# The output layer of a second MLP as seven block products, with its sums kept transposed

## The chip, the cores and the metric

The kernel runs on one core of one Trainium2 chip. The metric is the time of one execution on the device, in microseconds. Five engines work side by side, each through its own queue of instructions: TensorE (PE in the profile, with its weight loads as PEld), VectorE (DVE), ScalarE (ACT), GpSimd (POOL) and SyncE (SP), which here issues every transfer between HBM and SBUF. TensorE writes its results to PSUM, in banks of 128 x 512 numbers of 32 bits.

## The reference

Eight batches of 576 tokens go through an attention with 32 memory slots per head and then through two MLPs. All inputs come in 64 bits, and the arithmetic is carried to more than 32-bit matmul precision by splitting each operand into a high and a low part.

```python
x = attention(q, k, v, phi)                  # 4608 tokens x 512
h = x @ w_in                                 # 512 -> 2048
x = np.maximum(0.01 * h, h) @ w_out          # 2048 -> 512
gate = 1.0 / (1.0 + np.exp(-(x @ w_gate)))   # 512 -> 1536
val = x @ w_val                              # 512 -> 1536
out = (gate * val) @ w2_out                  # 1536 -> 512
```

## The kernel before

The first part (up to about 780 us) runs attention and the first MLP batch by batch. In the same time it converts the weights of the second MLP in the background (`stash_jobs`): each piece of 512 columns comes in as 64-bit words (`Piece`), is made a 32-bit number by ScalarE, VectorE and GpSimd, split into high and low, and stored to HBM, `w_gate` and `w_val` as `gvs`, `w2_out` as `w2s`. The result of the first MLP is stored transposed, as `x2s`.

The second MLP works on `PAIRS`: four pairs of 2 x 512 tokens and a fifth of 2 x 256 (`h` is 512 or 256). Its 1536 hidden features are cut into `NTH` = 3 parts `th` of `TH` = 4 blocks of 128. For each th there are four groups (`m2_group`: j = 0, 1; val = 0 for the gate, 1 for the value). A group multiplies a 2 x 2 block of weights with a 2 x 2 block of the input by the Strassen-Winograd scheme: seven products (`prod`) in place of eight. Each product is six matmuls: two halves of the contraction, and for each the three combinations high x high, low x high, high x low. The input's seven operands `xo` (block sums of x and their split) are made once per pair by `x_sums`, `x_hi` and `x_lo`. The weights' seven operands come from `gvs`, two to a tile `wt` of 512 KB (`w_load`, loaded whenever a tile comes free). The products land in PSUM banks `x`, `y`, `z`; ScalarE copies and VectorE additions put the four results together, the gate gets its sigmoid, and the value group multiplies with it and splits the product into `pt`.

The output layer (`m2_out`) follows the four groups of each th and is a plain product: for each chunk of 128 tokens, four blocks times three combinations accumulate 128 tokens x 512 features in a bank. The bank is copied (th = 0) or added (th = 1, 2) into `osum`; at the last th the chunk is stored by `store`. At the end of a stage the output weights of the next th, four tiles `w2t` of 512 KB, are loaded (`w2_load`). Between the chunks of a pair's last stage the next pair's `x_hi` and `x_lo` are issued (`between`), the low halves alternately to VectorE and GpSimd.

The order of the instructions is written out by hand: an engine does them as the program lists them. Memory is held in numbered slots: 16 slots `wo` (8 `pt` pairs, 4 `w2t`, 4 `osum`), 9 slots `vw` for `wt`; after the fourth pair seven more `wt` tiles are opened in the place of the x tiles, which are no longer wanted.

Of the kernel before, what the change touches and what calls it, by code (L numbers as in the profile page):

```python
# [119 lines left out]
def tile_kernel(  # L120
# [35 lines left out]
    NOP = 7  # L156
    NOPS = NF2 * NOP
    SCALE = 1.0 / float(D) ** 0.5

    const = ctx.enter_context(tc.tile_pool(name="const", bufs=1))  # L160
# [13 lines left out]
    w2s = dr.tile([P, NF2, 2, DM], F32, name="w2s")  # L174

    ident = const.tile([P, P], F32, name="ident")
    ones = const.tile([P, P], F32, name="ones")
    mask = const.tile([P, 4], F32, name="mask")
# [19 lines left out]
    class Piece:  # L198
# [12 lines left out]
        def a(self):  # L211
# [5 lines left out]
            self.k = cvp.tile([P, PC], F32, tag="k", name="k", bufs=4)  # L217
            nc.scalar.activation(self.y, w[:, :, 1].bitcast(F32), AF.Abs, scale=2.0 ** -3)
            nc.scalar.activation(self.k, w[:, :, 0], AF.Copy, scale=2.0 ** -27, bias=2.0 ** 25)
            if not self.late:  # L220
                self.sign()
            yield

        def sign(self):
            hi = self.raw.rearrange("p (n t) -> p n t", t=2)[:, :, 1]
            nc.scalar.activation(hi.bitcast(I32), hi.bitcast(F32), AF.Prelu, scale=2.0 ** -60, alpha=2.0 ** 120)  # L226

        def b(self):
            y = self.y
            nc.vector.tensor_scalar(y, y, 2.0 ** -18, 15359.998046875, op0=ALU.max, op1=ALU.min)  # L230
            if self.late:
                self.sign()
            yield
# [59 lines left out]
    def stash_jobs():  # L293
# [12 lines left out]
        def prep(key, o0):  # L306
            st = {}
            hl = {}

            def sums(n):  # L310
                fa, fb = (held[key, i].rearrange("p (a e f) -> p a e f", a=2, e=2) for i in range(2))
                a11, a12, a21, a22 = fa[:, :, 0], fa[:, :, 1], fb[:, :, 0], fb[:, :, 1]
                if n == 0:
                    t = ap_.tile([P, KD, HALF], F32, tag="pbuf", name="sums", bufs=1)
                    t = t.rearrange("p c f -> p (c f)")[:, 0:768].rearrange("p (k a f) -> p k a f", k=3, a=2)
                    s1, s2, s3, s4 = a21, t[:, 0], t[:, 1], t[:, 2]
# [11 lines left out]
            def hi(*ks):  # L328
                for k in ks:
                    hl[k] = cvp.tile([P, 2, 2, P], F32R, tag="k", name="hl", bufs=4)  # L330
                    nc.scalar.copy(hl[k][:, 0], st[k])
                    yield

            def lo(*ks):
                for k in ks:
                    t = hl.pop(k)
                    nc.vector.tensor_sub(t[:, 1], st[k], f32(t[:, 0]))
                    nc.sync.dma_start(out=gvs[:, o0 + k], in_=f32(t))
# [16 lines left out]
        def w2_job(fc):  # L355
            t = {}
            p, stages = conv(rows(w2_out, fc), lambda f: t.update(f=f))

            def hi():
                t["hi"] = cvp.tile([P, PC], F32R, tag="k", name="w2_hi", bufs=4)  # L360
                nc.scalar.copy(t["hi"], t["f"])
                nc.sync.dma_start(out=w2s[:, fc, 0], in_=f32(t["hi"]))
                yield

            def lo():
                t["lo"] = cvp.tile([P, PC], F32R, tag="k", name="w2_lo", bufs=4)
                nc.vector.tensor_sub(t["lo"], t["f"], f32(t["hi"]))
                nc.sync.dma_start(out=w2s[:, fc, 1], in_=f32(t["lo"]))
                yield

            return 3, p, stages + [hi, lo]

        for th in range(NTH):
            for j in range(TH // 2):
                for i, w in enumerate((w_gate, w_val)):
                    for e in range(2):
                        fc = TH * th + 2 * j + e
                        p, stages = conv(
                            w[:, fc * P:(fc + 1) * P].bitcast(U32).rearrange("(c p) f -> p c f", p=P),
                            lambda f, k=((th, j, i), e): held.update({k: f}),  # L380
                        )
                        yield (3 if e == 0 else 4), p, stages
# [482 lines left out]
    pt = []  # L865
    osum = []
    tmps = []
    n_tmp = [0]


    def x_open():
# [495 lines left out]
```

## Time and profile before

| | us |
|---|---|
| median of 3 executions | 1598.17 (1596.18 to 1598.4) |
| profiled execution, its own time | 1599.8 |
| its span, first to last instruction | 1597.9 |
| TensorE busy in the span | 1548.1 (97%) |
| VectorE busy | 818.9 (51%) |
| ScalarE busy | 707.0 (44%) |
| GpSimd busy | 431.1 (27%) |

Matmuls are pipelined: the duration of one in a list (389 ns for 512 columns) is longer than its share of the time. The distance between starts, read from the chain, is what counts. The granted clock of TensorE over the whole span is 0.990 of full speed.

### The profile page before, as it was taken

Reading aid. Unit: us, or ns where it says so; the run is one execution under the profiler, and the core shown is the slowest. Engines: PE = TensorE matmul, PEld = TensorE weight load, DVE = VectorE, ACT = ScalarE, POOL = GpSimd, SP = SyncE. Lnnn points to the kernel's source line nnn. Section 1 sums busy time; section 2 is a strip of 40 time slices with the busy share of each in tenths; the row PEclk is TensorE's granted clock in tenths of the full one; section 3 lists DMA queues with packets and bytes.
Section 4 is the critical chain, followed back from the end, with each engine's and each line's share of the span. In section 5 each row is a group of like instructions: output and inputs, shape, how many; then the busy total and the mean of one; then the engine's idle time right before and its main releaser. Section 6 shows DMA issues by size and latency. Waiting matters only on the chain.

```text
span 1597.9 us, 27449 instructions
## 1 busy us (share of the span) xinstructions
PE 1548.1 (97%) x10544; PEld 1358.2 (85%) x10544; DVE 818.9 (51%) x1426; ACT 707.0 (44%) x1602; POOL 431.1 (27%) x429
## 2 busy tenths in 40 slices
PE   4889999999999999999999999999999999999999
PEld 2677989989899998999988888888888888888898
DVE  6886444555554555432145475355535475255544
ACT  5875555665556555645333143223333133223332
POOL 2986344454455444533100020000200020000100
PEclk8799999999999999999999999999999999999999
DMA  9823554554556555323456447536557447537692
GB/s 301 283 53 85 142 142 138 164 140 141 155 153 186 140 160 155 106 82 109 143 162 223 142 152 235 194 111 223 195 162 223 143 149 236 169 109 224 224 395 77
DMA packets 203490, 268.66 MB, mean 168 GB/s; under 512 B 95072, under 2 KB 140128, under 8 KB 203360
## 3 DMA queue, kind: packets, MB, share of 16 engines
q1 hardware_dynamic: 203360, 266.92, 53.4%
q8 instruction: 83, 1.36, 0.4%
q14 instruction: 47, 0.39, 0.1%
HBM read 219.68 MB, written 47.19 MB: 167 GB/s over the span
## 4 chain that ended last, share of the span: by engine, by line
PE 82%; ACT 1%; DMA 1%; DVE 1%; issue 0%; POOL 0%; DVEq 0%; SPq 0%; ACTq 0%; POOLq 0%
PE acc L841 20%; PE oacc L1047 18%; PE ps_y L949 14%; PE ps_h L819 9%; PE ps_x L949 9%; PE ps_z L949 9%; PE ps_vw L789 1%; PE ps_kv L556 1%; DMA wt<-gvs 1%; PE ps_sc L631 0%; ACT gr L824 0%; ACT obuf L850 0%; DVE vw L801 0%; DVE t L536 0%; ACT raw L226 0%
## 5 line engine op out<-in xcount | busy, mean ns | idle before, releaser
L841 PE MATMUL acc<-gh,wo 128*128 128x288 f32 x2048 | 428.6, 301 | 3.2 <-ACT obuf L850 1.8
L841 PEld LDWEIGHTS acc<-gh,wo 128*128 128x128 f32 x2048 | 328.7, 189 | 27.3 <-issue 14.2
L188 POOL TENSOR_TENSOR gl<-gr,gh 128x288 fp32r<-128x288 f32 x250 | 217.9, 873 | 329.4 <-ACT gh L187 216.7
L841 PE MATMUL acc<-gl,wo 128*128 128x288 f32 x1024 | 304.9, 298 | 1.0 <-POOL gl L188 1.0
L1047 PE MATMUL oacc<-w2t,pt 128*128 128x512 f32 x1296 | 296.3, 389 | 0.0
L1047 PEld LDWEIGHTS oacc<-w2t,pt 128*128 128x128 f32 x1296 | 243.1, 188 | 50.3
L949 PE MATMUL ps_y<-xo,wt 128*128 128x512 f32 (+1 forms) x1080 | 252.0, 369 | 0.0
L949 PEld LDWEIGHTS ps_y<-xo,wt 128*128 128x128 f32 x1080 | 190.4, 188 | 33.8
L819 PE MATMUL ps_h<-at_hi,vw 128*128 128x288 f32 x1024 | 215.2, 298 | 3.5 <-ACT vw L187 2.7
L824 ACT ACTIVATE gr<-ps_h 128x288 f32<-128x288 f32 x256 | 105.4, 412 | 253.1 <-PE ps_h L819 228.9
L912 POOL TENSOR_TENSOR xo<-xr,xo 128x512 fp32r<-128x512 f32 (+1 forms) x16 | 23.0, 1458 | 671.0 <-ACT xo L908 671.0
L841 PEld LDWEIGHTS acc<-gl,wo 128*128 128x128 f32 x1024 | 193.9, 189 | 1.8 <-POOL gl L188 1.7
L819 PEld LDWEIGHTS ps_h<-at_hi,vw 128*128 128x128 f32 x1024 | 167.2, 191 | 5.0 <-ACT vw L187 3.6
L949 PE MATMUL ps_z<-xo,wt 128*128 128x512 f32 (+1 forms) x720 | 167.4, 368 | 1.0 <-DMA wt<-gvs 1.0
L949 PE MATMUL ps_x<-xo,wt 128*128 128x512 f32 (+1 forms) x720 | 167.5, 368 | 0.0
L819 PE MATMUL ps_h<-at_lo,vw 128*128 128x288 f32 x512 | 152.0, 297 | 0.0
L984 ACT CAST pt<-sg 128x512 fp32r<-128x512 f32 (+1 forms) x120 | 69.4, 578 | 182.1 <-DVE sg L977 182.1
L949 PEld LDWEIGHTS ps_z<-xo,wt 128*128 128x128 f32 x720 | 127.1, 189 | 23.5 <-DVE pt L981 1.2
L949 PEld LDWEIGHTS ps_x<-xo,wt 128*128 128x128 f32 x720 | 127.2, 188 | 22.9
L187 ACT CAST gh<-gr 128x288 fp32r<-128x288 f32 x256 | 111.8, 437 | 2.2
L819 PEld LDWEIGHTS ps_h<-at_lo,vw 128*128 128x128 f32 x512 | 97.4, 190 | 0.0
L996 ACT COPY tmp<-ps_x 128x512 f32<-128x512 f32 (+1 forms) x60 | 32.4, 541 | 136.7 <-PE ps_x L949 136.7
(176 smaller groups left out, 1703.1 us busy)
## 6 DMA issues: line engine op xcount, KB each, us to landing
wt<-gvs SPq DMA_DIRECT2D x210, 512.0 KB, 4.5
w2t<-w2s SPq DMA_DIRECT2D x60, 512.0 KB, 5.1
gvs<-hl SPq DMA_DIRECT2D x84, 256.0 KB, 2.5
x2s<-obuf SPq DMA_DIRECT2D x15, 576.0 KB, 3.8
win<-in_moe_w_in_dram SPq DMA_DIRECT2D x16, 512.0 KB, 9.7
wo_bits<-in_moe_w_out_dram SPq DMA_DIRECT2D x16, 512.0 KB, 10.4
xr<-x2s SPq DMA_DIRECT2D x16, 512.0 KB, 6.3
out_dram<-osum SPq DMA_DIRECT2D x32, 256.0 KB, 2.0
```

Of the source, the lines that this page charges most:

```text
L187: nc.scalar.copy(hi, raw)
L188: eng.tensor_sub(lo, raw, f32(hi))
L556: nc.tensor.matmul(p[M * h:M * h + M, 0:2 * D], a, x, start=(c == 0), stop=(c == CC))
L789: nc.tensor.matmul(ps[g][M * h:M * h + M, n * VB:(n + 1) * VB], kvT[b, g][D * g:D * g + D, 1, M * h:M * h + M], win[j][D * g:D * g + D, h, ...
L819: nc.tensor.matmul(p[:, :HALF], w, x, start=(n == 0), stop=(n == 3 * NG - 1))
L824: nc.scalar.activation(gr, p[:, :HALF], AF.Prelu, alpha=0.01)
L841: nc.tensor.matmul(a[d][:, :HALF], w[:, ds_], x, start=(open_ and n == 0), stop=(close and n == 2),)
L912: eng.tensor_sub(t[:, 1, :h], x_operand(n, k, a), f32(t[:, 0, :h]))
L949: nc.tensor.matmul(bank, w[:, l, a, :], x[:, r, :h], start=(start and i == 0), stop=(i == 5), skip_group_check=not start,)
L984: nc.scalar.copy(d[:, 0, :h], s)
L996: read(lambda: nc.scalar.copy(s1, x))
L1047: nc.tensor.matmul(bank[i], pt[2 * f + t][:, l, q * P:(q + 1) * P], w2t[f][:, r, :], start=(f == 0 and l + r == 0), stop=(f == TH - 1 and ...
```

## The change

- **Output layer.** `m2_out` also uses seven products. The weights of `w2_out` are prepared as seven block operands by the same `prep` as the others (`out_blocks`), with 32-column blocks interleaved, and stored in `w2s` so that one block of one product (256 KB: two j, high and low, 128 x 128) is one load. The weights are now the stationary operand and the tokens the moving one: a stage is 7 products x 2 halves (e) x 6 matmuls of h columns, with results of 128 features x h tokens, the transpose of what is stored.
- **Ring.** Four tiles of 256 KB (`ring`) are loaded in the order of use; each is loaded again right after the bank that used it. They take two slots `wo`; the 14 operands `ops` take the other 14. The sums take four slots `vw`, which leaves five for `wt`.
- **Operands.** A value group now writes seven operands per j (four products, three differences more) and splits them: `op_hi` on ScalarE, `op_lo` on VectorE, spread over the following banks by `after`. For the last group of a pair (`direct`) more of it is issued at once.
- **Running chains.** In a group, `y` takes products 0, 1, 4, 6 one after another without being cleared, and ScalarE copies its contents after 0, 1 and 4; `z` takes 2 and 5. In the output stage banks 0 and 1 take products 0, 1, 4, 6, banks 2 and 3 products 2 and 5, and then 3. Each content is copied or added into `sums` (`SUM_OF`).
- **Order.** The stage of th - 1 comes after the first group of the next th; the stage of the last th follows its groups at once. `x_sums` moves from the groups into the first th's stage, `x_hi` and `x_lo` into the last ten banks of the last stage, 11 of 14 low halves on GpSimd.
- **Output.** VectorE turns the sums back in blocks of 32 x 32 (`turns`: 16 instructions per pair of 1024 tokens), one at a time after banks and two at a time in gate groups (`lazy`), and four stores of 128 KB with runs of 512 bytes bring 256 tokens out. For this the rows of q in the first batch are read as (c p) in place of (p c).
- **First MLP.** `gh`, `gl` and `gr` become slices of fixed tiles; constants move into another pool; late pieces convert their low word one step later.

Not shown in the diff: the pools, the helper `ghl_next`, the slots of the temporaries, and the group's branches for `direct`.

```diff
-    w2s = dr.tile([P, NF2, 2, DM], F32, name="w2s")
+    IN_AT = IN_SEQ = (0, 2, 1, 3, 4, 5, 6)
+    OUT_SEQ = (0, 2, 1, 5, 4, 3, 6)
+    w2s = dr.tile([P, NTH, 2, NOP, TH // 2, 2, P], F32, name="w2s")
...
+        def out_blocks(x, y):
+            x, y = (t.rearrange("p (g i e r) -> p i e g r", i=2, e=2, r=32) for t in (x, y))
+            return x[:, 0], y[:, 0], x[:, 1], y[:, 1]
...
-                out=s["q"][:, c], in_=q[b, g, :, 0:SM, :].rearrange("h (p c) d -> c p h d", c=CC)[c],
+                out=s["q"][:, c], in_=q[b, g, :, 0:SM, :].rearrange("h (c p) d -> c p h d", c=CC)[c],
...
+    def w2_load(t):
+        x = next(r_next, None)
+        if x:
+            th, e, k = x
+            nc.sync.dma_start(out=f32(t), in_=w2s[:, th, e, k])
+            r_at.append(t)
+
+    def read(*todo, turns=0):
+        for op in todo:
+            op()
+        n_read[0] += 1
+        for op in later.pop(n_read[0], []):
+            op()
+        for _ in range(turns):
+            if lazy:
+                lazy.pop(0)()
...
         y = ps_a.tile([P, 512], F32, tag="a", name="ps_y")[:, :h]
-        prod(1, y, True)
-        u2 = new()
-        read(lambda: nc.vector.tensor_add(u2, y, s1))
+        prod(0, y, True)
+        read(copy(c11, y), turns=turns)
         yield
         z = ps_h.tile([P, 512], F32, tag="h", name="ps_z")[:, :h]
         prod(2, z, True)
+        read(copy(c22, z), turns=turns)
+        yield
+        prod(1, y, False)
+        read(copy(c12, y), turns=turns)
+        yield
+        x = ps_h.tile([P, 512], F32, tag="h", name="ps_x")[:, :h]
+        prod(3, x, True)
+        read(add(c11, x, c11), turns=turns)
...
+        for k in OUT_SEQ:
+            for e in range(2):
+                start = k in (0, 2, 3)
+                b = banks[e if k in (0, 1, 4, 6) else 2 + e][:, :h]
+                w = r_at.pop(0)
+                i = 0
+                for j in range(TH // 2):
+                    for l, r in ((0, 0), (0, 1), (1, 0)):
+                        nc.tensor.matmul(
+                            b, w[:, j, l, :], ops[j][k][:, r, :h], start=(start and i == 0), stop=(i == 5),
+                            skip_group_check=not start,
+                        )
+                        i += 1
+                w2_load(w)
+                o = sums[SUM_OF[k]][:, e, :h]
+                if th == 0 and k in (0, 2, 1, 6):
+                    read(lambda: nc.scalar.copy(o, b), turns=1)
+                else:
+                    read(lambda: nc.vector.tensor_add(o, b, o), turns=1)
+                for f in between.pop(0) if between else ():
+                    f()
...
+                        if th > 0 and (j, val) == (0, 0):
+                            sums_ = [] if th > 1 or not more else [(n + 1, a, i) for a in range(2) for i in range(4)]
+                            m2_out(n, th - 1, [[]] * 5 + [[lambda o=o: x_sums(*o)] for o in sums_])
...
+            m2_out(n, NTH - 1, between)
+            if n + 2 == len(PAIRS):
+                w_free.extend(p2[0].tile([P, 2 * PC], F32R, tag="xr", name="wt", bufs=7) for _ in xr + xt)
+                w_load()
```

## Rows read from the trace of the kernel before

**Rows 1.** Windows: start:end, length, busy us (count) per engine, granted clock, DMA share, GB/s.
```profile
200.00:400.00 200.00, 195.06 (x1842) 182.43 (x1841) 102.38 (x198) 115.40 (x304) 95.76 (x104) 0.99 0.50 145
...
600.00:780.00 180.00, 179.20 (x1585) 170.92 (x1584) 59.79 (x111) 93.68 (x238) 76.45 (x84) 1.00 0.34 108
780.00:1498.10 718.10, 718.10 (x3179) 595.27 (x3179) 367.09 (x555) 218.21 (x380) 38.97 (x28) 1.00 0.56 179
1498.10:1597.90 99.80, 94.80 (x649) 88.10 (x647) 48.05 (x117) 28.99 (x76) 0.00 (x0) 1.00 0.67 256
```

**Rows 2.** Chain of waits, output stages: start us, length us, what.
```profile
818.14 21.76 PE oacc L1047 x96
877.98 21.76 PE oacc L1047 x96
...
1519.74 10.91 PE oacc L1047 x48
```

**Rows 3.** Chain of waits, 1490 to 1530 us, the fifth pair's first products.
```profile
1502.16 8.47 DMA wt<-gvs
1510.63 0.14 issue
...
1512.42 0.72 PE ps_y L949 x6
```

**Rows 4.** Transfers of the page: count, size, median us from issue to landing.
```profile
wt<-gvs SPq DMA_DIRECT2D x210, 512.0 KB, 4.5
...
out_dram<-osum SPq DMA_DIRECT2D x32, 256.0 KB, 2.0
...
ph<-in_phi_dram SPq DMA_DIRECT2D x16, 256.0 KB, 4.4
```

**Rows 5.** Transfers issued from 1017.4 to 1017.6 us.
```profile
w2t<-w2s SPq DMA_DIRECT2D x1, 512.0 KB, 3.6
```

**Rows 6.** SyncE's instructions in order, 1476 to 1530 us.
```profile
1476.41 0.32 SPq L918 DMA_DIRECT2D wt<-gvs  x1
...
1502.16 24.20 SPq L918 DMA_DIRECT2D wt<-gvs  x21
```

**Rows 7.** Transfers issued from 1502 to 1520 us.
```profile
wt<-gvs SPq DMA_DIRECT2D x16, 512.0 KB, 10.2
```

**Rows 8.** Windows of the fifth pair, columns as in rows 1.
```profile
1498.10:1519.74 21.64, 20.64 (x170) 20.45 (x169) 11.92 (x30) 7.79 (x21) 0.00 (x0) 1.00 0.92 342
1519.74:1530.65 10.91, 10.91 (x51) 9.02 (x50) 2.71 (x8) 2.98 (x6) 0.00 (x0) 1.00 1.03 410
```

**Rows 9.** VectorE's instructions in order, 1117 to 1140 and 1540 to 1552 us.
```profile
1118.57 0.68 DVE L977 TENSOR_TENSOR sg<-sg,tmp 128x512 f32<-128x512 f32 x1
1119.17 0.68 DVE L1030 TENSOR_TENSOR tmp<-ps_y,tmp 128x512 f32<-128x512 f32 x1
...
1126.11 0.68 DVE L1058 TENSOR_TENSOR osum<-oacc,osum 128x512 f32<-128x512 f32 x1
1126.71 1.19 DVE L912 TENSOR_TENSOR xo<-xt,xo 128x512 fp32r<-128x512 f32 x1
...
1541.75 0.42 DVE L977 TENSOR_TENSOR sg<-sg,tmp 128x256 f32<-128x256 f32 x1
1542.09 0.42 DVE L1030 TENSOR_TENSOR tmp<-ps_y,tmp 128x256 f32<-128x256 f32 x1
```

**Rows 10.** Groups by line and shape: busy us, mean ns of one, idle before.
```profile
L996 ACT COPY tmp<-ps_x 128x512 f32<-128x512 f32 x48 | 28.1, 586 | 114.1 <-PE ps_x L949 114.1
...
L912 POOL TENSOR_TENSOR xo<-xr,xo 128x512 fp32r<-128x512 f32 x12 | 19.5, 1651 | 503.1 <-ACT xo L908 503.1
...
L641 DVE STREAM_TRANSPOSE e<-ps_sc 128x288 f32<-128x288 f32 x28 | 13.0, 473 | 11.9 <-PE ps_sc L631 11.9
```

**Rows 11.** All engines in order, 1593 to 1598 us.
```profile
1592.83 1.07 PE L1047 MATMUL oacc<-w2t,pt 128*128 128x512 f32 x4
...
1593.93 0.69 DVE L1058 TENSOR_TENSOR osum<-oacc,osum 128x512 f32<-128x512 f32 x1 [0.67 <-PE oacc L1047]
```

## What I predict, and how the numbers come about

> **What bounds the kernel now.** I read the busy time of each engine by stage first. From 200 us on TensorE is busy nearly all the time: 195 of 200 us early in the first MLP, 718.1 of 718.1 us in the first four pairs of the second MLP and 94.8 of 99.8 us in the fifth pair, at a granted clock of 0.99 to 1.00 [rows 1]. VectorE and ScalarE are about half idle there (367 and 218 of 718 us). The chain of waits comes second: it shows how regular the second MLP is [rows 2]. An output stage of 96 matmuls takes 21.76 us, and the next one starts 59.84 us after the last, so 38.08 us hold the 168 matmuls of four groups. Both come to 226.7 ns for 512 columns, with no gap. In the fifth pair an output stage is 48 matmuls of 512 columns in 10.91 us, and six matmuls of 256 columns take 0.72 us [rows 3]: 120 ns each. So a matmul taken away is time taken away, as long as what feeds TensorE keeps up. The rest of the reading asks that: how fast VectorE and ScalarE work off a queue, and how fast a block of weights lands.
>
> **What the change removes from TensorE.** An output stage goes from 8 chunks x 4 x 3 = 96 matmuls to 7 products x 2 halves x 6 = 84 of 512 columns. Twelve stages in the first four pairs: 144 x 226.7 ns = **-32.6 us**. In the fifth pair the moving side is now 256 tokens wide: 144 matmuls at 227.3 ns (32.7 us) become 252 at 120 ns (30.2 us): **-2.5 us**. The groups keep their 168 matmuls.
>
> **The ring of output weights, first four pairs.** Four tiles of 256 KB take the place of four of 512 KB that were loaded a whole th ahead. The load for bank i+4 is issued when bank i's six matmuls are done, and has three banks, 3 x 1.36 = 4.08 us, to land. The trace has no such load. Its neighbours: a 256 KB store lands in 2.0 us, a 512 KB tile of group weights in 4.5 us [rows 4], the first of a burst of four output-weight loads, 512 KB, in 3.6 us [rows 5]; a landing reaches TensorE 0.14 us later [rows 3]. I take 2.9 us, about half way between 2.0 and 3.6: 3.04 us against 4.08, so **0**. Bounds: 0, and with 4.5 us 0.56 us late at the fifth, ninth and thirteenth bank of 12 stages, 36 x 0.56 = +20.
>
> The Trainium skill (DMA: Bandwidth & Descriptors, Anatomy of one DMA) gives a fixed 2.0 us or so and bytes over 436 GB/s for a transfer; by it, as an estimate, the load would take 2.6 us, which is nothing in this term and 4 us less in the next one. That the fixed part stays when the piece is halved speaks against this ring; the rows agree in that the 256 KB store still takes 2.0 us.
>
> **The ring, fifth pair.** A bank is 0.72 us there, so the cover is 2.16 us and a load of 2.9 + 0.14 us is 0.88 us late. Three late points in each of three stages, less the first, which is the next term: 8 x 0.88 = **+7.0**. Bounds: 0 at 2.0 us, 8 x 2.48 = +20 at 4.5 us.
>
> **The queue ahead of the fifth pair's first output stage.** When pair 3 ends, seven more tiles of group weights are opened and loaded at once, as before. Before, that filled the transfer engines: after 1502 us loads were issued back to back on SyncE [rows 6], each landed after 10.2 us [rows 7], and 410 GB/s moved while TensorE waited only 1.0 us of 21.64 [rows 8], because 16 tiles were held or on the way and no output weights were wanted in a hurry: the four of the next th had been asked for at the end of the stage before. After, the first output stage comes after five groups, 5 x 5.16 = 25.8 us (20.64 us for four [rows 8]), and its ring loads queue on SyncE behind everything issued by then: 7 tiles, 17.5 tiles freed by the five groups, and pair 3's output stores, which move from that pair's end into these groups. At 410 GB/s a tile costs 1.28 us: 24.5 x 1.28 + 2.1 MB / 410 GB/s = 31.3 + 5.1 = 36.4 us. The queue is 10.6 us behind when the stage begins, and its fifth bank waits about that long (the load's own landing and its cover cancel within 1 us): **+10.6**. Bounds: if the groups take 1 us longer each and the stores pass unnoticed, 0.5. The stores now go in runs of 512 bytes, and 256 KB of phi in such runs land in 4.4 us against 2.0 for a store in long runs [rows 4]: eight times 2.4 us more, less the queue's overlap, gives up to +25.
>
> **VectorE and ScalarE.** Per pair of 1024 tokens VectorE goes from 139 instructions (36 in each th's groups, 16 bank sums, 8 sums and 7 splits for the next pair) to 187 (42 in each th's groups, 34 bank sums, 16 transposes, 8 and 3), ScalarE from 94 (24 a th, 8 bank copies, 14 casts) to 136 (38 a th, 8, 14). In a queue that never empties VectorE starts a 512-column instruction every 0.605 us, a 256-column one every 0.34 us, and those that read PSUM are as fast beside a busy GpSimd (0.68 us), while a split between two SBUF tiles grows to 1.19 us [rows 9]. 187 x 0.605 = 113 us in a pair of 3 x 57.1 = 171 us; ScalarE at 0.59 us [rows 10] 80 us. On the mean both lie beside TensorE. The dense place is the last group of a pair, whose seven operands go straight into the output stage. From the fifth product's end at 6.8 us (the group's start is 0) VectorE has ten instructions until the third product's operand is split at 12.7 us; TensorE wants it at 13.1 us. Behind these, seven splits and differences and the first bank sums share the queue, and each bank is summed before it is wanted again. No stall by this count, 0.4 us of room. I take 0.5 us at each of five such places and 0.5 us elsewhere: **+3**. Bounds 0 and, at 2 us each, +10. GpSimd gets 11 of 14 splits of the next pair instead of 7, at 1.65 us apiece [rows 10]; they have 19 us of output stage and then a product of 1.36 us for every two.
>
> **Ends.** Before, 4.0 us pass from the last matmul (1593.9 us [rows 11]) to the span's end: a sum and a store. After: a sum (0.42 [rows 9]), four transposes of 256 columns (0.44 each by the 0.473 us of one of 288 [rows 10]), four store issues (0.32 each [rows 6]), the landing (2.0 [rows 4]) and some 0.5 us of hand-overs: 6.0 us, **+2.0**. The 1.0 us wait for weights at the fifth pair's start: **-1.0**.
>
> **First MLP.** Six preparations of output weights add 24 sums, 30 splits, 30 casts and 18 stores on VectorE, ScalarE and SyncE. VectorE is busy 102 of 200 us and 60 of 180 us there [rows 1]; some 27 us more in 540 us is hidden. 0, bounds -3 and +3. The other moves (slices of one tile in place of pools, the order in which q's rows of the first batch are read) leave every count as it was: 0.
>
> **Sum.** -32.6 - 2.5 + 0 + 7.0 + 10.6 + 3 + 2.0 - 1.0 = -13.5 us, against the profiled execution's own 1599.8 us: **1586.3 us**. That execution is 1.6 us above the median shown (0.1%), which is inside what I call no change: 0.2%, 3.2 us, is about what a measurement of this kernel can tell.
>
> **The rivals.**
> - *The queue does no harm* (0.22). The ring's loads find idle engines, the first stage waits 1 us, later banks 4 us in all, VectorE 1 us: -32.6 - 2.5 + 1 + 4 + 1 + 2 - 1 = -28 us, **1572 us**. For it: before, TensorE waited only 1.0 us in the same stretch. Against it: loads of 10.2 us there.
> - *The ring is late everywhere* (0.10), the other side: a 256 KB block lands no sooner than a 512 KB tile, at 4.5 us. Then +20 in the first four pairs and +13 more in the fifth: **1619 us**. It decides from a landing of 4.1 us. For it: 4.5 us in the same kind of stretch; against it: 3.6 us for the burst's first.
> - *The new chain on ScalarE and VectorE holds TensorE* (0.08): each accumulation into a running bank waits for a copy of what it held, behind whatever ScalarE waits for. 0.4 us in each of 60 groups is 24 us in place of 3: **1607 us**; slower from 0.3 us each. Against it: 47 to 66% load and 1.36 us between a copy and the next use.
> - *The fifth pair gives it all back* (0.16): stores in small runs cost the full +25: **1601 us**. The Trainium skill (TensorE: Matmul & The Clock Gate, Part 1) adds that an idle array falls from 2.4 to 1.2 GHz, so a wait of this length would be followed by matmuls at half speed; before, the granted clock stays 1.00 there, with no wait long enough to show it.
> - My sum as it stands (0.44), 1577 to 1597 us.
>
> **How the numbers follow.** 1586 us is the likeliest case. The range runs from 1567, below the first rival, to 1607: it leaves out the late ring, half of the chain and the lowest part of the first. Faster: nearly all of my case, the first rival and a quarter of the last, 0.68; same: half of the last and a little of mine, 0.10; slower 0.22.
>
> **What would show it.** Output stages of 84 matmuls in 19.0 us with a period of 57.1 us prove the first term and the ring's cover; a period near 58.8 us means the ring is late. The landing of the 256 KB loads decides: under 2 us the fifth pair is nearly free, at 3 us it has short waits every fourth bank. A wait of some 10 us at its first output stage, by TensorE for a ring block, is the queue. Waits of TensorE or of its weight loads for ScalarE would be the chain. I am wrong if the fifth pair takes under 105 us or the first four save less than 25 us.

## The result, and the profile after

The changed kernel takes 1609.38 us, the median of four executions (1607.29 to 1610.8), against 1598.29 us (1596.18 to 1598.76) for the kernel before beside it: a ratio of 1.0071, with an interval of 1.0053 to 1.0088. It is slower by 0.7%, and 2.4 us above the range that was given. The profiled execution took 1610.8 us, its span 1609.0 us (before: 1597.9), at a granted clock of 0.982 (before: 0.990).

The windows by stage come first, columns as in [rows 1]:

```profile
200.00:400.00 200.00, 192.80 (x1815) 179.19 (x1814) 110.75 (x220) 117.74 (x312) 97.05 (x102) 0.99 0.51 151
600.00:780.00 180.00, 177.66 (x1570) 168.98 (x1569) 72.89 (x130) 93.56 (x243) 77.66 (x86) 0.99 0.31 94
1477.50:1518.50 41.00, 28.11 (x212) 27.49 (x211) 21.78 (x62) 15.13 (x44) 0.00 (x0) 0.83 0.97 328
1518.50:1535.90 17.40, 12.56 (x86) 11.75 (x85) 2.94 (x8) 3.41 (x10) 0.00 (x0) 0.90 0.78 276
...
1557.40:1571.60 14.20, 10.91 (x86) 10.21 (x85) 5.90 (x15) 0.77 (x3) 0.00 (x0) 1.00 0.74 242
1571.60:1609.00 37.40, 28.11 (x212) 26.04 (x210) 22.79 (x62) 10.74 (x30) 0.00 (x0) 0.93 0.41 121
1479.50:1500.00 20.50, 7.97 (x54) 7.77 (x53) 5.02 (x15) 3.08 (x10) 0.00 (x0) 0.70 1.03 344
826.12:1477.50 651.38, 650.48 (x2856) 534.92 (x2856) 432.33 (x704) 286.35 (x512) 55.15 (x44) 1.00 0.67 214
```

The last line is the first four pairs from the end of their first four groups on, 651.4 us. Before, that end is the first output stage of [rows 2], 818.14, and the fifth pair's first product comes at 1498.1 [rows 1]: 680.0 us for the same groups and stages. TensorE still has no gap worth naming there: the one wait found for it is 0.4 us, for a ring block in the very first stage. The fifth pair, from 1477.50 to the end, takes 131.5 us where it took 99.8, and in the first four of its windows shown TensorE is busy for 69 to 77% of the time. The line of 1479.5 to 1500 us is the worst stretch of its first groups, at a granted clock of 0.70. In the two windows of the first MLP it is busy for about 2 us less than in [rows 1].

Where the first MLP ends is read from the matmuls of its last accumulator `acc` between 770 and 810 us: shapes, first and last start. The first line is of the changed kernel, the second of the kernel before:

```profile
L854 PE MATMUL acc<-ghl,wo x99: 288/296/311, 769.8 to 793.2; 128*128 128x288 f32 x99
```

```profile
L841 PE MATMUL acc<-gl,wo x20: 288/294/310, 770.6 to 785.2; 128*128 128x288 f32 x20
```

793.2 against 785.2: the first MLP ends 8 us later. The next mark agrees: the first four groups end at 826.12, which is the first output stage in the chain below (835.64) less one group of 9.52 us, since a fifth group now stands ahead of that stage; before it was 818.14.

The account of the spans: first MLP **+8.0**, first four pairs **-28.6**, fifth pair with its tail **+31.7**: +11.1 us, from 1597.9 to 1609.0.

The chain of waits in the first four pairs, columns as in [rows 2]:

```profile
835.64 1.38 PE oacc L1133 x6
...
893.40 19.04 PE oacc L1133 x84
...
1008.61 19.09 PE oacc L1133 x84
...
1065.78 19.04 PE oacc L1133 x84
```

A stage of 84 matmuls takes 19.04 us where [rows 2] shows 21.76 for 96, and from 1008.61 to 1065.78 the period is 57.17 us. The same view in the fifth pair, around its first groups and at its first output stage:

```profile
1479.02 8.25 DMA wt<-gvs
1487.28 6.42 DMA out_dram<-turned
...
1493.82 0.77 DVE turned L1120 x2
...
1496.65 1.65 PE ps_y L999 x6
1498.30 1.28 PE ps_x L999 x6
1499.58 1.29 PE ps_y L999 x6
...
1519.39 5.79 DMA ring<-w2s
```

SyncE's instructions at the first place, in order, show what the two transfers at 1479 and 1487 us are:

```profile
1478.11 3.90 SPq L937 DMA_DIRECT2D wt<-gvs  x7
1482.06 5.54 SPq L1173 DMA_DIRECT2D out_dram<-turned  x4
```

And the waits between 1478 and 1500 us (who waited for whom: us in total, times, longest):

```profile
DVE turned L1120 <- DMA out_dram<-turned: 13.6, 2, 12.8
ACT sg L1023 <- DVE tmp L1029: 13.5, 2, 13.0
PEld ps_y L999 <- ACT tmp L1032: 12.7, 1, 12.7
PE ps_y L999 <- ACT tmp L1032: 12.5, 1, 12.5
```

This is one wait handed on three times. The seven extra tiles of weights are issued first; the stores of the pair before are issued behind them and land late. There are two staging tiles `turned`, so VectorE's next transpose, issued in a gate group two at a time, stands still until a store has landed. Behind it on VectorE is an addition that ScalarE wants for the sigmoid, and behind that sigmoid on ScalarE is the copy of a bank that TensorE wants to reuse. TensorE stops for 12.5 us for a store with which it has nothing to do.

The transfers of the page:

```profile
ring<-w2s SPq DMA_DIRECT2D x210, 256.0 KB, 2.9
...
out_dram<-turned SPq DMA_DIRECT2D x72, 128.0 KB, 2.9
```

And the end, all engines in order:

```profile
1599.78 1.66 PE L1133 MATMUL oacc<-op,ring 128*128 128x256 f32 x12 [0.19 <-DMA ring<-w2s]
...
1601.81 1.74 DVE L1120 STREAM_TRANSPOSE turned<-sum 128x256 f32<-128x256 f32 x5
1602.27 3.92 SPq L1173 DMA_DIRECT2D out_dram<-turned  x8
```

The last matmul ends at 1601.4 us, the span at 1609.0: 7.6 us where it was 4.0.

### The profile page after: what moved, and what is told of

The parts are those of the page before. It is cut to its first block, busy times and chain, and to the rows that moved or that the text cites. A ratio compares the mean times of both kernels' runs of the same rounds, so it can differ in the third digit from the quotient of the medians.

```text
span 1609.0 us, 28276 instructions
## 1 busy us (share of the span) xinstructions
PE 1529.6 (95%) x10508; PEld 1339.6 (83%) x10508; DVE 953.4 (59%) x1724; ACT 820.1 (51%) x1846; POOL 449.4 (28%) x445
## 4 chain that ended last, share of the span: by engine, by line
PE 71%; DVE 6%; DMA 3%; ACT 3%; issue 1%; SPq 0%; DVEq 0%; ACTq 0%
PE acc L854 18%; PE ps_y L999 17%; PE oacc L1133 12%; PE ps_h L833 8%; PE ps_z L999 8%; PE ps_x L999 4%; DMA ring<-w2s 1%; PE ps_vw L803 1%; DVE op L1017 1%; DVE sum L1143 1%; PE ps_kv L570 1%; DVE sg L1020 1%; ACT op L1013 1%; DVE sg L1026 1%; DVE tmp L1029 1%
## 5 line engine op out<-in xcount | busy, mean ns | idle before, releaser
L854 PE MATMUL acc<-ghl,wo 128*128 128x288 f32 x3072 | 466.7, 301 | 6.4 <-POOL ghl L186 2.2
L854 PEld LDWEIGHTS acc<-ghl,wo 128*128 128x128 f32 x3072 | 424.3, 190 | 33.1 <-issue 13.4
L999 PE MATMUL ps_y<-xo,wt 128*128 128x512 f32 (+1 forms) x1440 | 330.1, 370 | 13.7 <-ACT tmp L1032 13.6
L186 POOL TENSOR_TENSOR ghl<-grs,ghl 128x288 fp32r<-128x288 f32 x250 | 217.8, 873 | 339.4 <-ACT ghl L185 256.5
L1133 PE MATMUL oacc<-op,ring 128*128 128x512 f32 (+1 forms) x1260 | 270.1, 372 | 10.5 <-DMA ring<-w2s 8.5
L1133 PEld LDWEIGHTS oacc<-op,ring 128*128 128x128 f32 x1260 | 221.0, 190 | 57.3 <-DVE sum L1143 8.0
L837 ACT ACTIVATE grs<-ps_h 128x288 f32<-128x288 f32 x256 | 105.5, 412 | 251.5 <-PE ps_h L833 223.3
L1143 DVE TENSOR_TENSOR sum<-oacc,sum 128x512 f32<-128x512 f32 (+1 forms) x170 | 106.8, 635 | 105.5 <-PE oacc L1133 104.7
L1013 ACT CAST op<-sg 128x512 fp32r<-128x512 f32 (+1 forms) x180 | 103.5, 579 | 77.1 <-DVE sg L1020 47.9
L185 ACT CAST ghl<-grs 128x288 fp32r<-128x288 f32 x256 | 111.7, 436 | 2.0
L1017 DVE TENSOR_TENSOR op<-sg,op 128x512 fp32r<-128x512 f32 (+1 forms) x180 | 111.6, 643 | 0.5
```

Of the source, the lines that this page charges most:

```text
L185: nc.scalar.copy(hi, raw)
L186: eng.tensor_sub(lo, raw, f32(hi))
L837: nc.scalar.activation(gr, p[:, :HALF], AF.Prelu, alpha=0.01)
L854: nc.tensor.matmul(a[d][:, :HALF], w[:, ds_], x, start=(open_ and n == 0), stop=(close and n == 2),)
L999: nc.tensor.matmul(bank, w[:, l, a, :], x[:, r, :h], start=(start and i == 0), stop=(i == 5), skip_group_check=not start,)
L1013: return lambda: nc.scalar.copy(ops[j][k][:, 0, :h], x)
```

## The experiments

Each ran beside the kernel before on its chip, whose medians were 1598.6 to 1600.0 us. Where one time is given, the kernel ran once, and its stages are read rather than its total: "first MLP" is the last start of `acc` against 785.2 us of before, and the fifth pair is split into its five groups ahead of the first output stage (ideal 25.8 us), its stages (ideal 10.1 us each) and the rest. In the changed kernel these are +8.0; 41.0; 17.4, 14.3; and 21.5 us for the last stage (13.9) with the tail.

**late_open.** The seven extra tiles are opened three groups into the fifth pair.

```diff
+    if (n + 1, th, j, val) == (len(PAIRS), 0, 1, 0):
+        w_free.extend(p2[0].tile([P, 2 * PC], F32R, tag="xr", name="wt", bufs=7) for _ in xr + xt)
+        w_load()
...
-            if n + 2 == len(PAIRS):
-                w_free.extend(p2[0].tile([P, 2 * PC], F32R, tag="xr", name="wt", bufs=7) for _ in xr + xt)
-                w_load()
```

> One edit: the seven extra weight tiles of the fifth pair are opened after its second gate group instead of before its first group. Theory A (the seven loads of 3.7 MB stand in the transfer queue ahead of pair 3's output stores; the stores free the two staging tiles late; VectorE's transposes wait for them and hold up everything behind them, 12.5 us of TensorE waiting for ScalarE): the 12.5 us wait shrinks to under 4 us and the low clock after it goes, so the fifth pair takes 115 to 120 us instead of 131.5 and the whole 1594 to 1599 us. Rival B (the stores themselves, in runs of 512 bytes and two staging tiles, are too slow whatever stands ahead of them): the wait stays above 8 us and the whole above 1603 us.

1611.3 us, no gain. The groups fell to 33.4 us and VectorE's long wait for a store from 12.8 to 2.5 us, so the mechanism was the one supposed; but the first stage grew to 24.3 us. Its chain:

```profile
1504.18 10.48 DMA wt<-gvs
...
1514.72 9.57 DMA ring<-w2s
...
1524.42 4.19 PE oacc L1133 x18
```

The ring's load now queues behind the moved tiles and holds TensorE for 9.8 us: the term that I had priced at 10.6 us, at the place where I had put it, though with the tiles opened three groups later than in the sum. The time was not saved, it changed its name.

**slow_turns.** In the fifth pair one transpose is issued after each product, in place of two in gate groups alone: `turns = 1 if n + 1 == len(PAIRS) else 0 if val else 2`.

> One edit: in the fifth pair's groups one lazy instruction (transpose or store) is issued after every product, in place of two after each product of gate groups. The seven loads stay where they are. Theory A: the transposes still come to a staging tile whose store stands behind 3.7 MB of weights; the wait is only moved by a few products, and 6 to 12 us of it stay: 1603 to 1609 us. Rival B (two transposes per 0.72 us product are simply too dense for VectorE): the wait is gone and the whole comes to 1594 to 1598 us.

1612.63 us, above both ranges, with the first MLP 11.3 us late; the groups stay at 41.0 us. TensorE's largest wait falls to 7.3 us and comes later, and smaller ones make up for it; VectorE still waits for the landing of a store (11.2 us at the longest). Spreading the transposes does not help while the stores land late.

**ring_deep.** Four of the seven tiles become eight more blocks of the ring, opened at the same point.

```diff
+                xs = [p2[0].tile([P, 2 * PC], F32R, tag="xr", name="wt", bufs=7) for _ in xr + xt]
+                for t in xs[:4]:
+                    t = t.rearrange("p (i j l f) -> p i j l f", i=2, j=TH // 2, l=2)
+                    for i in range(2):
+                        w2_load(t[:, i])
+                w_free.extend(xs[4:])
```

> One edit: of the seven extra tiles of the fifth pair four become eight more ring blocks (12 in place of 4) and three become weight tiles; they are opened at the same point as before. Theory (a 256 KB block takes 2.9 us to land against 2.16 us of cover, and queues behind weight tiles at the first stage): the three output stages of the fifth pair fall from 17.4, 14.3 and about 14 us to about 10.3 us each, 14 us less, so about 1595 us; the 12.5 us wait in the first group stays. Rival (the stages are late because VectorE's bank sums and the operands are late): the stages shrink by less than 4 us in all, 1605 us or more.

1595.81 us. Windows of its groups, its long wait and two of its stages:

```profile
1477.00:1517.40 40.40, 28.36 (x212) 27.90 (x211) 21.81 (x62) 15.02 (x44) 0.00 (x0) 0.83 0.96 329
1483.40:1495.50 12.10, 0.33 (x4) 0.13 (x2) 2.07 (x6) 1.20 (x4) 0.00 (x0) 0.67 1.06 388
1517.40:1527.50 10.10, 10.10 (x87) 10.10 (x86) 2.95 (x8) 3.42 (x10) 0.00 (x0) 1.00 1.04 398
1548.90:1559.00 10.10, 10.10 (x87) 10.10 (x86) 5.95 (x15) 0.82 (x3) 0.00 (x0) 1.00 0.98 348
```

With twelve blocks the stages are TensorE alone, busy for 10.10 of 10.10 us, and the last stage with the tail falls by 2.3 to 19.2 us. The long wait stays as it was, 12.1 us with the transfers at 1.06 busy. So the two losses of the fifth pair are separate: the ring's depth holds the stages, the stores behind the loads hold the groups.

**fifth_all.** The deep ring, opened three groups later, one transpose after each product, and two after each bank of the very last stage.

> Late opening, one lazy instruction after every product, twelve ring blocks, and two lazy instructions after each bank of the very last stage. If the fifth pair's excess is the queue (12.5 us and the low clock), the ring (14 us) and the tail (2 us), the pair goes from 131.5 to 101 to 106 us and the whole to 1579 to 1585 us, ratio to before 0.988 to 0.992. If the copies on ScalarE and the sums on VectorE bound its groups, the pair stays above 112 us and the whole above 1590 us.

1593.57 us over ten executions, ratio 0.9972 (0.9962 to 0.9982); 1579 to 1585 was expected. The stages are at their 10.07 us, but the groups still take 39.8 us, in several waits of 1 to 4 us for weights. The transfers are 98.5% busy from 1475 to 1515 us, where 13.3 MB pass.

**bare_w2.** The preparations of the output weights leave out their sums, casts and splits; the pieces are stored as they are, so that the output is computed from other weights.

```diff
-                yield 4, None, prep((th, j, i), blocks, dst)
+                yield 4, None, prep((th, j, i), blocks, dst) if i < 2 else bare((th, j, i), dst)
```

> Left out: the block sums, high copies and low splits of the output weights in the background of the first MLP; the converted pieces themselves are stored, with the same 42 stores at the same steps, so the output is computed from other weights. Everything else as in the changed kernel. Theory A (the extra casts and splits, which share four buffers with the conversions and wait for stores to land, make ScalarE late for the first MLP's own work): the first MLP ends where it ended before, 7 to 8 us earlier, 1601 to 1602 us. Rival B (fixed slices for gh, gl, gr): nothing moves, 1608 to 1610 us. Rival C (the stores on SyncE ahead of the attention's loads): nothing moves either, since they stay.

1609.39 us, first MLP +6.1. Seven kernels that leave the first MLP as the change made it end it 6.1 to 11.3 us late (8.0, 8.6, 11.3, 7.0, 6.1, 7.9, 10.2), so this is no gain outside that scatter: nothing shows the added arithmetic as the cost. The edit also takes no buffer of tag `k` for these blocks, so their own share of that tag is not shown as the cost either; but their pieces are held until their stores have landed.

**slices_before.** The kernel before, with `gh`, `gl` and `gr` as slices of fixed tiles, as the change has them.

> The kernel before with one part of the change: gh, gl and gr as slices of fixed tiles. Theory A: no change, 1597 to 1600 us. Rival B: the first MLP gets 8 us longer, 1605 to 1607 us.

1598.97 us, first MLP -0.6: the slices cost nothing.

**low_first.** The changed kernel, with the low word of a late piece converted one step earlier, as before.

> One part of the change undone: in background pieces the low word is again converted one step earlier, and the sign step comes after it. Theory A (buffers of the shared tag are what is short): the low word holds a buffer for one step longer, so the first MLP gets no shorter and perhaps 1 to 4 us longer, 1609 to 1613 us. Rival (the new order itself costs the time): the first MLP ends up to 8 us earlier, 1601 to 1603 us.

1618.76 us, first MLP +11.7, just past the scatter's upper edge. The later conversion costs nothing; it may gain a little.

**k5.** A fifth buffer for the tag `k`, which holds the low words of pieces, and prepared blocks until their stores have landed (4 to 5 in both its users); the room comes from `ghl`, cut to its 6 x `HALF`, with the staging tiles moved.

```diff
-            self.k = cvp.tile([P, PC], F32, tag="k", name="k", bufs=4)
+            self.k = cvp.tile([P, PC], F32, tag="k", name="k", bufs=5)
```

> One edit to the changed kernel: five in place of four buffers for the tag that the low words and the high/low pairs of the background share (its memory comes from smaller tiles; the two staging tiles of the output move). Its first MLP ends 8 us later than before's in the profile, 6 to 11 us in the runs so far. Theory A (ScalarE waits for a buffer of this tag, which is freed by the landing of a store): the first MLP ends 4 to 8 us earlier than in the changed kernel, under 3 us behind before. Rival B (the denser cadence of the background work, or its transfers on SyncE): it ends 6 us or more behind before, as in all runs so far.

1606.19 us. The accumulator's last matmul comes 6.7 us earlier than in the changed kernel:

```profile
L854 PE MATMUL acc<-ghl,wo x67: 288/295/310, 769.8 to 786.5; 128*128 128x288 f32 x67
```

First MLP +1.3, well outside the scatter. The rest of this kernel is 2 us slower than the changed one's.

**cadence.** The gate and value preparations take five slots each in place of four: `yield (5 if i < 2 else 4), None, prep(...)`.

> One edit to the changed kernel: five in place of four steps of the first MLP for each preparation of gate and value weights, the distance that it had before. Theory B (12 preparations packed closer): the first MLP ends 1 to 4 us behind before. Theory A (the shared buffers) allows some of that too, since stores get more time to land; no gain, 6 us or more behind, speaks against both and for the number of conversions and stores.

1611.44 us, first MLP +5.9: at the edge of the scatter, no gain to rely on.

**cadence_before.** The kernel before, with the background work in the change's denser cadence and nothing else.

```diff
-                        yield (3 if e == 0 else 4), p, stages
-                    yield 5, None, prep((th, j, i), NOP * (TH * th + 2 * j + i))
+                        yield (2 if e == 0 else 4), p, stages
+                    yield 4, None, prep((th, j, i), NOP * (TH * th + 2 * j + i))
```

> The kernel before with the new distances of the background work (2, 4, 4 steps in place of 3, 4, 5 for gate and value weights), the rest as it was. If the cadence alone costs the time, the first MLP ends 4 us or more later than before's and the whole is 1602 us or more; if it is the added work on the output weights, it ends within 2 us and the whole is 1597 to 1600 us.

1612.25 us. Its accumulator, with no preparation of output weights at all:

```profile
L841 PE MATMUL acc<-gl,wo x40: 288/295/310, 770.8 to 797.5; 128*128 128x288 f32 x40
```

+12.3 us. In the kernel before, the denser cadence alone costs at least what the whole change costs in this stage. Its waits between 180 and 700 us name the path:

```profile
ACT k L219 <- DMA gvs<-hl: 8.1, 4, 3.1
...
PE ps_sc L631 <- ACT kvT L613: 7.0, 3, 3.5
```

At 403.8 us ScalarE has stood still for 3.1 us until a store of `gvs` had landed and a buffer of tag `k` was free, and at 405.4 us TensorE has waited 3.5 us for ScalarE; the same comes again at 498 us. In the kernel before, ScalarE waits 1.3 us in all at that place, and TensorE's wait is not in its list.

**fifth_v2.** Three transposes after each bank at the end of the fourth pair, so that its stores go out ahead; of the seven tiles two are opened as four more ring blocks after the fourth group, and five for group weights after the first stage. One transpose follows each product of the fifth pair, two each bank of its last stage.

```diff
+        pops = 3 if last and n + 2 == len(PAIRS) else 2 if last and end else 1
...
+                        if (n + 1, th, j, val) == (len(PAIRS), 0, 1, 1):
+                            for t in more_[:2]:
...
+                            if (n + 1, th) == (len(PAIRS), 1):
+                                w_free.extend(more_[2:])
+                                w_load()
```

> The fifth pair rearranged once more: three lazy instructions after each of the last banks of pair 3's last stage, so that two of its four stores are issued before the fifth pair; one after each product there; four more ring blocks opened after the fourth group and five weight tiles after the first output stage. In the run with late opening and twelve blocks, the transfer engines were 98% busy from 1475 to 1515 us and moved 13.4 MB, so TensorE waited for weights. If that stretch is bound by transfers, moving 1 MB of stores ahead and 4.7 MB of early loads behind takes its groups from 39.8 to 27 to 32 us and the whole to 1582 to 1588 us; if the stores' small runs hold it, the groups stay above 36 us.

1596.08 us over six executions, ratio 0.9975 (0.996 to 0.999); 1582 to 1588 was expected. The groups come to 32.3 us, but the first two stages take 14.2 and 15.6, with waits of 2.4 and 3.8 us for a ring block: eight blocks, four of them asked for late, are not enough.

**never_open.** The seven tiles are never opened: the five tiles `wt` and the four blocks of the ring hold the weights of the fifth pair too.

> The seven extra weight tiles of the fifth pair are never opened: five weight tiles and four ring blocks serve it to the end, so 3.7 MB less is loaded ahead. Theory A (those loads, all at once, are what delays first the stores and then the ring): the 12.8 us wait in the first group falls under 4 us and the 4 us wait at the first output stage's fifth bank under 2 us, with short waits of 1 to 1.5 us at the ring's late banks left; the five groups take 27 to 31 us, the first stage 12 to 14 us, the fifth pair 112 to 118 us instead of 131.5. Rival B (the fifth pair needs more weights ahead than five tiles hold, and the stores take their time anyway): its groups get long waits for weights, the pair takes 125 us or more.

1606.78 us, fifth pair 125.7 us, where 112 to 118 was expected; that is the rival's total, though the groups' waits for weights are 1.45 us at the longest. The longest wait in the first groups falls from 12.8 to 2.8 us and the first stage from 17.4 to 14.8: the loads are the cause of the one and of a part of the other. The second stage takes 17.9 us, with a wait of 3.05 for a ring block, after which 42 matmuls take 8.25 us (at 120 ns each 5.0; the granted clock of this stage is 0.81): the ring of four is late there even with no burst ahead of it.

**combined.** The fifth buffer; the last stage of the fourth pair with three transposes after a bank; one after each product in the fifth pair; two after each bank of the very last stage; four extra tiles opened one by one as ring blocks after its second to fifth group, the other three as weight tiles after the first stage.

```diff
+                        if n + 1 == len(PAIRS) and (th, j, val) in ((0, 0, 1), (0, 1, 0), (0, 1, 1), (1, 0, 0)):
+                            t = more_.pop().rearrange("p (i j l f) -> p i j l f", i=2, j=TH // 2, l=2)
+                            for i in range(2):
+                                w2_load(t[:, i])
...
+                            if (n + 1, th) == (len(PAIRS), 1):
+                                w_free.extend(more_)
+                                w_load()
```

> Five shared buffers in the first MLP, three lazy instructions per bank at the end of pair 3 and one per product in the fifth pair, four extra tiles opened one after another as eight ring blocks between its second and fifth group, three as weight tiles after its first output stage, two lazy instructions per bank in the very last stage. If the costs found so far add up (first MLP 1 to 2 us behind before, four pairs 28.6 us ahead, fifth pair 105 to 110 us against 99.8): 1576 to 1583 us, ratio 0.986 to 0.990. If the fifth pair is held by transfers in small runs whatever their order: it stays at 115 us or more and the whole at 1586 us or more.

**1583.3 us** over four executions (1582.6 to 1583.55), ratio 0.990 (0.9883 to 0.9916) to 1599.2 of the kernel before: it is 1% faster than the kernel before, and faster than the changed one too. Windows of the fifth pair:

```profile
1472.00:1505.70 33.70, 28.15 (x212) 27.03 (x212) 21.15 (x60) 15.40 (x45) 0.00 (x0) 0.95 1.01 348
1505.70:1515.80 10.10, 10.10 (x87) 10.10 (x86) 2.80 (x7) 3.27 (x10) 0.00 (x0) 1.00 1.03 391
1537.50:1547.50 10.00, 10.00 (x86) 10.00 (x85) 5.91 (x15) 0.78 (x3) 0.00 (x0) 1.00 1.04 396
1547.50:1581.70 34.20, 26.91 (x212) 25.69 (x210) 22.30 (x62) 10.73 (x30) 0.00 (x0) 0.94 0.43 140
```

Against before: first MLP +2.4, first four pairs -28.5, fifth pair +9.9 (109.7 us): -16.2 us. The stages are whole; the first five groups are still 8 us over their ideal, with the transfers at 1.01 busy and 348 GB/s.

## Why the prediction was wrong

The forecast was -13.5 us, and the spans differ by +11.1: 24.6 us apart. The first MLP holds 8.0 of them, the first four pairs 1.5 (-28.6 where the matmuls and five sixths of VectorE's term make -30.1), the fifth pair with its tail 15.1 (+31.7 for +16.6).

- **Matmuls taken away: right.** 19.04 us a stage and a period of 57.17 are what "what would show it" names. The first four pairs gave 28.6 of the 32.6 us.
- **Ring in the first four pairs: right.** The landing is 2.9 us in the median of all blocks, the value taken, and the cover of 4.08 us held in all stages but the first, which waits 0.4 us. The Trainium skill (DMA: Bandwidth & Descriptors, Anatomy of one DMA) gives its fit for transfers issued by GpSimd; the 2.6 us worked out from it, an estimate, is 0.3 us short of these loads, which SyncE issues. The estimate changes nothing here, and in the fifth pair's term it would be 2.4 us less (8 x 0.58 = 4.6 in place of 7.0), not the 4 us that the prediction names. The rival of the late ring would have begun at a landing of 3.9 us, 4.08 less the 0.14 of the sum, and not at 4.1.
- **VectorE and ScalarE: right, a little low.** 32.6 less 28.6 is 4.0 us against 2.5 for these pairs. The last stage of a pair takes 20.0 us in place of 19.04, and the first stage of all 19.7, of which the 0.4 us for the ring block are a part.
- **Ring and queue in the fifth pair: right in sum by luck, both terms mis-sized.** 7.0 + 10.6 was predicted; the three stages are 7.3, 4.2 and 3.8 us over, together 15.3. The queue holds the fifth bank of the first stage for 3.8 us (the load at 1519.39 in the chain above, less its cover), not 10.6. The groups ahead of it had taken 41.0 us in place of 25.8, so the queue had 15 us more to empty. That the loss which the sum left out hid most of the one that it had follows from this, but no run shows it by itself; late_open, with the tiles opened later and the groups at 33.4 us, has such a queue with 9.8 us. The ring costs more than predicted: the second and third stage are 8.0 us over where 6 x 0.88 = 5.3 was counted, and in never_open, with no burst ahead, the first two alone are 4.7 and 7.8 over, the low clock after a wait included.
- **The fifth pair's groups: the missing term.** The working put the fourth pair's stores into SyncE's queue and asked who waits for the ring. It did not ask who waits for the *stores*. Their landing frees the two staging tiles, VectorE needs one for its next transpose, and ScalarE and TensorE are queued behind VectorE. 15.2 us of the loss lie in its first five groups (41.0 for 25.8): the wait of 12.5 us, and the slow products after it, for the most part. ring_deep kept this loss while it removed the other, late_open and never_open took its wait from 12.8 to under 3 us.
- **The rival "gives it all back"** had the right place, small stores in the fifth pair, and nearly the total for that pair: 99.8 + 16.6 + 14.4 = 130.8 us, 131.5 measured. It had the wrong way: not the stores' own duration but their place behind 3.7 MB of loads. Its remark on the clock came true: after the wait six matmuls of 256 columns take 1.28 us in place of 0.72 [rows 3], and the granted clock is 0.70 from 1479.5 to 1500 us and 0.50 from 1492 us on, the lower of the two levels. The Trainium skill (TensorE: Matmul & The Clock Gate, Part 1) says that an idle array falls to 1.2 GHz; this trace agrees. Three products, 1.65, 1.28 and 1.29 us in place of 0.72 each, make 2.1 us.
- **Ends: mis-sized.** +2.0 was predicted, +3.6 measured. Five transposes were still to do, in 1.74 us, and eight stores were issued at 0.49 us each, where four at 0.32 were counted.
- **First MLP: the step that failed by argument.** I costed the added work at nothing because VectorE has time beside it, with bounds of 3 us; the first MLP became 8.0 us longer. Engine time was the wrong measure. k5 and combined (+1.3 and +2.4) show that a fifth buffer of tag `k` takes most of it back, bare_w2 that leaving out the added arithmetic gives nothing back that can be told from the scatter, and cadence_before that in the kernel before the denser cadence costs this much with no added work. These buffers are freed by the landing of a store, so the reading that fits is that the cadence is bound by buffers in flight. In cadence_before such a wait is seen to reach TensorE. In the changed kernel ScalarE waits for such a landing too, as here at 305 us:

```profile
305.13 0.31 ACT hl L334
...
305.48 4.20 DMA w2s<-hl
...
309.76 0.41 ACT hl L334
```

Its place is on a chain with TensorE's matmuls, because ScalarE stands still with the splits of `ghl` behind it.

Three things stay open. The waits of ScalarE for such landings between 180 and 700 us do not grow in sum from before (14.7 us) to after (13.1), though they are 18.8 in cadence_before and 7.2 in k5, so which of them reach TensorE in the changed kernel was not settled. Nor does it lose its time where cadence_before does: that kernel's TensorE is short between 400 and 500 us (busy 92.5 of 100, before 98.3, after 99.2), the changed kernel's between 300 and 400 us (95.8, before 98.7) and 600 and 700 us (97.7, before 99.2). That the cadence is the cause in the changed kernel is therefore argued, not shown; that the number of buffers is, k5 and combined show. Why kernels with an unchanged first MLP differ by 5 us in its end was not settled either; ten executions of one kernel, fifth_all, lie 5.0 us apart as well. And the 8 us that combined still loses in its first five groups were not told apart into transfers and order.

My own test for being wrong looked for a fifth pair under 105 us. It took 131.5: I had looked for the failure on the side of the gain alone.

## What to carry to other kernels

When a step puts a transfer behind others, ask of it not only who wants its data but what its landing frees, and follow that buffer through every engine that stands in line for it: with two staging tiles a late store stopped VectorE, ScalarE and TensorE in turn. Background work that ends in stores can be limited by buffers in flight while its engines have time to spare: here a fifth buffer took 5.6 to 6.7 of 8 us back, so raise the cadence and add a buffer together. And a cure that moves loads moves the wait with them (late_open); here a deeper ring, loads given out piece by piece, earlier stores and the fifth buffer together gave 26 us, where the deeper ring alone had given 13.6 in its one run. A sum that comes out for two terms together proves neither: here one came out too small and the other too large.

## What the runs showed of the hardware that was not expected

- A store of 128 KB behind 3.7 MB of loads on the same issuing engine paid twice: by the chain it left SyncE at 1487.28, when a load of 8.25 us had landed, and then took 6.42 us itself, against a median of 2.9.
- After 12.5 us of rest eighteen matmuls of 256 columns took 4.2 us in place of 2.2, at a granted clock of 0.50 from 1492 to 1500 us; in never_open, after a wait of 3.05 us, 42 took 8.25 us in place of 5.0. These waits cost more than their length.
- Eight store issues back to back took 0.49 us each on SyncE for 128 KB in runs of 512 bytes; a single load of 512 KB took 0.32 [rows 6], but seven such loads back to back 0.56 each (the line at 1478.11), so the small runs are not shown as the cause.
